# A lightweight convolution and a gated feed-forward: the first 1024 tokens convolved with channels as output partitions

## The chip, the cores and the metric

The kernel runs on one core of one Trainium2 chip. The metric is the device time of one execution in microseconds (us); the lower the better. Engines are named as in the profile: PE (TensorE matmuls), PEld (its weight loads), DVE (VectorE), ACT (ScalarE), POOL (GpSimd) and SP (SyncE, which here only issues DMAs).

## The reference

The input `x` has 8 batches of 4096 tokens with 192 channels. Each of 8 heads owns 24 channels and has 7 taps, made by a softmax. Every token becomes the weighted sum of itself and its six predecessors; then all 32768 tokens go through a gated feed-forward.

```python
w = weight - np.max(weight, axis=-1, keepdims=True)      # weight: (8, 7)
w = np.exp(w)
w = w / (np.sum(w, axis=-1, keepdims=True) + 1e-09)
x_pad = np.concatenate([np.zeros((B, 6, D)), x], axis=1)  # x: (8, 4096, 192)
idx = np.arange(S)[:, None] + np.arange(7)[None, :]
x_unf = x_pad[:, idx, :].reshape(B, S, 7, 8, 24)
y = np.einsum('hk,bskhg->bshg', w, x_unf).reshape(B * S, D)
gate = np.maximum(y @ w_gate, 0.0)                        # (192, 1536)
val = y @ w_val                                           # (192, 1536)
return (gate * val @ w_out).astype(np.float32)            # (1536, 192)
```

## The kernel before

The four pairs of batches (bp and bp + 4) go one after the other; in each pair the two batches are the two streams `st`, whose data lie on the lower and the upper 64 partitions. The unit of the feed-forward is a window of 512 tokens of both streams; a pair of batches has eight windows.

The convolution is a matmul with a band matrix: 118 tokens (112 and the 6 before them) in, 112 out, one 118 x 112 band for each head. The bands of heads 0 to 3 and 4 to 7 are two tiles, built at the start from the softmax (L163 to L201): DVE makes `prod` and `blk`, and ten small copies by DVE and ACT (L199, L201) put `blk` along the diagonals. Blocks of 112 tokens form groups: the first group of a batch has five, the others four. `load_x` (L88) brings one group of both streams into a tile `x_h` with GpSimd DMAs that turn fp32 into fp16; `xpool` has four such tiles, so a load waits for the convolution four groups earlier. The first tokens of a batch have no predecessors: a memset on DVE (L97) clears the rows ahead of them.

There are two forms of the convolution. `conv` (L255) has the band as the stationary operand: 8 matmuls (L266), one a head, whose output has tokens as partitions. ACT (three copies) and DVE (two) move it to a tile `y` (L279), and SP transposes each block by DMA (L298) into `xc`, which has channels as partitions, as the feed-forward needs it. `conv_first` (L215) serves only the first group of the program. It has `x_h` as the stationary operand in pieces of at most 32 channels, so that its output has channels as partitions at once: 120 matmuls (L238) into two PSUM tiles, then three copies to `xc` (L248 on ACT, L249 on DVE, L250 on ACT), and no transpose.

`gate_val` (L303) takes a window through 12 steps f of 128 hidden units each: 6 matmuls with Wg, 6 with Wv (L314), ReLU on ACT (L324), product on DVE (L325). `project` (L328) is 48 matmuls with Wo (L332), a copy by ACT (L340) and a store by SP (L342), for one stream of one window. PSUM holds four tiles of two banks each (`ps`), taken in turn by all of these.

The order is written out by hand. Windows go in twos: both `gate_val`, then the four `project`, and a `conv` after each `project` as long as a later window needs it, with a load of x behind it. In the first window two `conv` calls stand ahead of steps f = 4 and f = 8:

```python
            if bp == 0 and w == 0 and f in (4, 8):
                conv(0, f // 4)
```

The weights are needed on both halves of the partitions. A DMA brings them to the lower half in four slices of 384 hidden units (`load_w`, L141), a copy doubles them into the upper half (`both_halves`, L148): slice 0 on DVE, slices 1 to 3 on POOL. All these DMAs, all loads of x and the load of Wo (L364) are issued by POOL, in the order of the program, with its copies among them:

```python
    load_w(0)
    load_w(1)
    xts[1] = load_x(0, 1)
    load_w(2)
    xts[2] = load_x(0, 2)
    load_w(3)
    for s in range(1, NPART):
        both_halves(nc.gpsimd, s)
```

At the very start, while nothing is loaded yet, PE runs 24 matmuls on zeros (L77).

Of the kernel before, what the change touches and what calls it, by code (L numbers as in the profile page):

```python
# [8 lines left out]
FP = mybir.dt.float32  # L9
F16 = mybir.dt.float16  # L10
# [5 lines left out]
def kernel(  # L16
# [12 lines left out]
    nc = tc.nc  # L29

    B, S, D = x.shape
    H, KW = weight.shape
    G = D // H
    DFF = moe_w_gate.shape[1]
    PAD = KW - 1
    NB = B // 2
    NCH = D // 64
    NBLK = D // 32
    NFF = DFF // 128
    WIN = 512  # L40
    NWIN = S // WIN
    SUB = 112
    NSUB = (S + SUB - 1) // SUB
    GSUB = 5
    SUBS = [list(range(GSUB))] + [list(range(j, j + 4)) for j in range(GSUB, NSUB, 4)]
    NGRP = len(SUBS)

    ctx.enter_context(tc.manual_schedule())
    const = ctx.enter_context(tc.tile_pool(name="const", bufs=1))
    xpool = ctx.enter_context(tc.tile_pool(name="xpool", bufs=4))  # L50
    ypool = ctx.enter_context(tc.tile_pool(name="ypool", bufs=3))
    xcpool = ctx.enter_context(tc.tile_pool(name="xcpool", bufs=2))
# [2 lines left out]
    opool = ctx.enter_context(tc.tile_pool(name="opool", bufs=3))  # L55
    psum = ctx.enter_context(tc.tile_pool(name="psum", bufs=4, space=bass.MemoryType.PSUM))


    HH = H // 2
    wr = const.tile([128, HH, KW], FP)  # L60
    for half, eng in ((0, nc.sync), (1, nc.scalar)):
        eng.dma_start(
            out=wr[64 * half : 64 * half + 64],
            in_=bass.AP(
                tensor=weight.tensor,
                offset=weight.offset + half * HH * KW,
                ap=[[0, 64], [KW, HH], [1, KW]],
            ),
# [4 lines left out]
    zeros = const.tile([128, 512], F16)  # L73
    nc.vector.memset(zeros[:], 0.0)  # L74
    ps = psum.tile([128, 2, 512], FP, name="ps")
    for n in range(24):
        nc.tensor.matmul(  # L77
            out=ps[:, n % 2, :], lhsT=zeros[:, 0:128], rhs=zeros[:], start=True, stop=True
        )
# [2 lines left out]
    for half in range(2):  # L82
        nc.vector.memset(bands[half][:], 0.0)  # L83


    TOK = [min(SUB * j, S - SUB) for j in range(NSUB)]

    def load_x(bp, g):  # L88


        subs = SUBS[g]
        xt = xpool.tile([128, GSUB, 2, D], F16, name="x_h")
        for st in range(2):
            b = bp + NB * st
            jj = 0
            if g == 0:
                nc.vector.memset(xt[0:32, 0, st, :], 0.0)  # L97
                nc.gpsimd.dma_start(out=xt[PAD:128, 0, st, :], in_=x[b, 0 : 128 - PAD, :])  # L98
                jj = 1
            last = subs[-1] == NSUB - 1  # L100
            n_full = len(subs) - jj - int(last)
            lo = TOK[subs[jj]] - PAD
            src = bass.AP(
                tensor=x.tensor,
                offset=x.offset + (b * S + lo) * D,
                ap=[[D, 128], [SUB * D, n_full], [1, D]],
            )
            nc.gpsimd.dma_start(out=xt[:, jj : jj + n_full, st, :], in_=src)  # L108
            if last:
                nc.gpsimd.dma_start(  # L110
                    out=xt[0 : SUB + PAD, len(subs) - 1, st, :], in_=x[b, S - SUB - PAD : S, :]
                )
        return xt, subs

    xts = {}
    xts[0] = load_x(0, 0)


    eye = const.tile([128, 32 + KW], FP)
    for half in range(2):  # L120
        nc.gpsimd.affine_select(  # L121
            out=eye[64 * half : 64 * half + 64],
            in_=ones[64 * half : 64 * half + 64],
# [9 lines left out]
    Wg = const.tile([128, NCH, DFF], F16)  # L133
    Wv = const.tile([128, NCH, DFF], F16)
    Wo = const.tile([128, NFF, D], F16)
    NPART = 4
    FS = DFF // NPART

    def load_w(s):
        for src, dst in ((moe_w_gate, Wg), (moe_w_val, Wv)):  # L140
            nc.gpsimd.dma_start(  # L141
                out=dst[0:64, :, FS * s : FS * (s + 1)],
                in_=src.rearrange("(c p) f -> p c f", p=64)[:, :, FS * s : FS * (s + 1)],
            )

    def both_halves(eng, s):
        for dst in (Wg, Wv):
            eng.tensor_copy(  # L148
                out=dst[64:128, :, FS * s : FS * (s + 1)], in_=dst[0:64, :, FS * s : FS * (s + 1)]
            )  # L150

    load_w(0)
    load_w(1)
    xts[1] = load_x(0, 1)
    load_w(2)
    xts[2] = load_x(0, 2)
    load_w(3)
    for s in range(1, NPART):
        both_halves(nc.gpsimd, s)


    mx = const.tile([128, HH, 1], FP)
# [20 lines left out]
        out=prod[:],  # L183
# [9 lines left out]
    for half in range(2):  # L193
        for n, (r0, b0, b1, s0) in enumerate(places):
            ncol = min(32, SUB - s0)
            src = blk[64 * half + b0 : 64 * half + b1, :, 0:ncol, 0]
            dst = bands[half][r0 : r0 + b1 - b0, :, s0 : s0 + ncol]
            if n % 2 == half:
                nc.vector.tensor_copy(out=dst, in_=src)  # L199
            else:  # L200
                nc.scalar.copy(out=dst, in_=src)  # L201

    def band(h):
        return bands[h // HH][0 : SUB + PAD, h % HH, :]

    both_halves(nc.vector, 0)

    xc = {}

# [2 lines left out]
    PLACE = {0: (0, 0, 0), 1: (0, 0, 1), 3: (0, 1, 0), 4: (0, 1, 1)}  # L212
    PLACE |= {6: (1, 0, 0), 7: (1, 0, 1), 2: (1, 1, 0), 5: (1, 1, 1)}

    def conv_first():  # L215


        xt, subs = xts.pop(0)
        xc[0] = xcpool.tile([128, NCH, S], F16, name="xc")
        n = 4  # L220
        rows = SUB + PAD
        pa = psum.tile([128, 2, 512], FP, name="ps")
        pb = psum.tile([128, 2, 512], FP, name="ps")
        places = [(pa, 0), (pa, 1), (pb, 0)]
        for c in range(NCH):
            for jj in range(GSUB):
                if jj < n:
                    ps, bank, col = *places[c], SUB * jj
                else:
                    ps, bank, col = pb, 1, SUB * c  # L230
                for second in range(2):
                    for st in range(2):
                        for k2 in range(2):
                            k = 2 * c + k2
                            h0, h1 = 32 * k // G, (32 * k + 31) // G
                            h, m = (h0, G * h1 - 32 * k) if second else (h1, 32)
                            p0 = 64 * st + 32 * k2
                            nc.tensor.matmul(  # L238
                                out=ps[p0 : p0 + m, bank, col : col + SUB],
                                lhsT=xt[0:rows, jj, st, 32 * k : 32 * k + m],  # L240
                                rhs=band(h),
                                start=True,
                                stop=True,
                                tile_position=(0, p0),
                                skip_group_check=True,
                            )
            if c == 1:
                nc.scalar.copy(out=xc[0][:, 0:2, 0 : n * SUB], in_=pa[:, :, 0 : n * SUB])  # L248
        nc.vector.tensor_copy(out=xc[0][:, 2, 0 : n * SUB], in_=pb[:, 0, 0 : n * SUB])  # L249
        nc.scalar.copy(  # L250
            out=xc[0][:, :, n * SUB : GSUB * SUB],
            in_=pb[:, 1, 0 : NCH * SUB].rearrange("p (c t) -> p c t", c=NCH),
        )

    def conv(bp, g):  # L255


        xt, subs = xts.pop(NGRP * bp + g)
        if g == 0:
            xc[bp] = xcpool.tile([128, NCH, S], F16, name="xc")  # L260
        n = len(subs)
        rows = SUB + PAD
        W = 2 * n * G
        pair = [psum.tile([128, 2, 512], FP, name="ps") for _ in range(2)]
# [29 lines left out]
        move(nc.scalar.copy, 1, 0, 0, 0, 2, 16, G, G)  # L294
        move(nc.vector.tensor_copy, 1, 1, 0, 8, 0, 48, 2 * 128 - 48, 16)
        move(nc.vector.tensor_copy, 1, 1, 16, -16, 1, 0, 56, 8)
        for jj, j in enumerate(subs):
            nc.sync.dma_start_transpose(  # L298
                out=xc[bp][:, :, TOK[j] : TOK[j] + SUB],
                in_=y[0:SUB, jj].rearrange("p c s r -> p (c s r)"),  # L300
            )

    def gate_val(bp, w):  # L303
        h = hpool.tile([128, NFF, 2, WIN], F16, name="hT")
        xcb = xc[bp]
        for f in range(NFF):
            if bp == 0 and w == 0 and f in (4, 8):
                conv(0, f // 4)
            pss = []
            for W in (Wg, Wv):  # L310
                ps = psum.tile([128, 2, 512], FP, name="ps")
# [33 lines left out]
        )  # L345


    groups = [(bp, g) for bp in range(NB) for g in range(NGRP)]
    need = []
    for bp in range(NB):  # L350
        for w in range(NWIN):
            sub = (WIN * (w + 1) - 1) // SUB
            need.append(NGRP * bp + next(g for g in range(NGRP) if sub in SUBS[g]))
    wins = [(bp, w) for bp in range(NB) for w in range(NWIN)]
    loaded = 3
    conv_first()
    done = 3
    for i in range(0, len(wins), 2):
        last = need[min(i + 4, len(wins) - 1)]
        while loaded <= min(last, done + 3):  # L360
            xts[loaded] = load_x(*groups[loaded])
            loaded += 1
        if i == 0:
            nc.gpsimd.dma_start(out=Wo[:], in_=moe_w_out.rearrange("(c p) d -> p c d", p=128))  # L364
        pair = [(*wins[i + j], gate_val(*wins[i + j])) for j in range(2)]
        for bp, w, h in pair:
            for st in range(2):
                project(bp, w, h, st)
                if done <= last and done < loaded:
                    conv(*groups[done])  # L370
                    done += 1
                    if loaded <= last:
                        xts[loaded] = load_x(*groups[loaded])
                        loaded += 1


# [28 lines left out]
```

## Time and profile before

| | |
|---|---|
| median of 3 runs | 805.76 us (805.64 to 806.78) |
| the profiled execution: time, span | 806.04 us, 804.1 us |
| mean granted TensorE clock | 0.994 |
| PE busy | 791.8 us (98%), 8104 matmuls |
| DVE busy, ACT busy, POOL busy | 498.7 us (62%), 487.7 us (61%), 76.1 us (9%) |
| L314 matmuls (gate and val) | 4608 |
| L332 matmuls (projection) | 3072 |
| L266 matmuls (`conv`) | 280 |
| L238 matmuls (`conv_first`) | 120 |

All times within the profile are microseconds from the span's start. Matmuls overlap in the array, so the duration of one is longer than the distance to the next; distances are read from the starts. The granted clock is a share of full speed. The time of an execution is somewhat longer than its span, which goes from the first to the last instruction. The span of a DMA issue on POOL is the time in which the engine writes its descriptors; the transfer itself ends later ("landing").

### The profile page before, as it was taken

What the parts mean: (1) busy time and instruction counts of PE and PEld (TensorE: products, weight loads), DVE (VectorE), ACT (ScalarE), POOL (GpSimd) and SP (SyncE); (2) the same over time, 40 slices, a digit from 0 to 9 for tenths busy, and PEclk for the clock granted to TensorE, in tenths of its full rate; (3) what the DMA queues carried; (4) which work ended last, traced back from release to release, by engine and by line L of the source; (5) the groups of instructions that cost most, each with busy time, mean ns of one, the idle gap of its engine ahead of it and who ended that gap; (6) DMA issues with size and microseconds to landing.
All of it is one profiled execution on the core that took longest, in us unless ns stands there. A gap on an engine that the chain in (4) does not pass through costs nothing.

```text
span 804.1 us, 18844 instructions
## 1 busy us (share of the span) xinstructions
PE 791.8 (98%) x8104; PEld 523.6 (65%) x8104; DVE 498.7 (62%) x482; ACT 487.7 (61%) x562; POOL 76.1 (9%) x109
## 2 busy tenths in 40 slices
PE   8799999999999999999999999999999999999997
PEld 3367494765947658485674947658485584856647
DVE  5663928659195682937749295591946839386490
ACT  3565737567475664747657375574747657375571
POOL 8401020000201002010010100201010010000000
PEclk9999999999999999999999999999999999999999
DMA  9909036160913209252090511908156070210202
GB/s 124 140 11 161 5 80 99 33 128 1 139 53 54 81 1 124 56 73 86 20 170 2 90 45 30 150 2 114 45 59 133 2 133 1 66 49 23 75 1 79
DMA packets 129170, 54.97 MB, mean 68 GB/s; under 512 B 94784, under 2 KB 129088, under 8 KB 129088
## 3 DMA queue, kind: packets, MB, share of 16 engines
q1 hardware_dynamic: 86496, 37.50, 20.2%
q0 software_dynamic: 42512, 16.28, 19.3%
q8 instruction: 63, 1.03, 0.5%
q14 instruction: 19, 0.16, 0.1%
q10 hardware_dynamic: 80, 0.01, 0.0%
HBM read 32.55 MB, written 25.17 MB: 72 GB/s over the span
## 4 chain that ended last, share of the span: by engine, by line
PE 97%; DMA 2%; POOL 0%; DVE 0%; ACT 0%; issue 0%; POOLq 0%; ACTq 0%
PE ps L314 62%; PE ps L332 32%; PE ps L266 3%; DMA xc<-y 1%; DMA Wv<-in_moe_w_val_dram 1%; POOL x_h L108 0%; POOL x_h L98 0%; ACT out_s L340 0%; DVE xc L249 0%; POOL Wg L141 0%; DVE Wv L148 0%; DVE band L83 0%; POOL eye L121 0%; ACT xc L250 0%; DVE zeros L74 0%
## 5 line engine op out<-in xcount | busy, mean ns | idle before, releaser
L325 DVE TENSOR_TENSOR hT<-gr,ps 128x1024 f16<-128x1024 f16 x384 | 468.9, 1221 | 142.0 <-ACT gr L324 107.1
L324 ACT ACTIVATE gr<-ps 128x1024 f16<-128x1024 f32 x384 | 392.8, 1023 | 108.2 <-PE ps L314 108.2
L314 PE MATMUL ps<-xc,Wg 64*128 64x512 f16 x2304 | 313.9, 378 | 6.3 <-DMA xc<-y 4.2
L314 PE MATMUL ps<-xc,Wv 64*128 64x512 f16 x2304 | 313.3, 378 | 0.0
L332 PE MATMUL ps<-Wo,hT 128*128 128x192 f16 x3072 | 261.7, 246 | 0.0
L332 PEld LDWEIGHTS <-hT 128*128 128x128 f16 x3072 | 253.2, 98 | 6.8 <-issue 6.8
L314 PEld LDWEIGHTS <-Wv 64*128 64x128 f16 x2304 | 130.7, 94 | 119.8 <-issue 2.4
L314 PEld LDWEIGHTS <-Wg 64*128 64x128 f16 x2304 | 112.0, 94 | 141.7 <-issue 8.3
L340 ACT COPY out_s<-ps 128x768 f32<-128x768 f32 x64 | 51.1, 798 | 195.5 <-PE ps L332 184.6
L279 DVE CAST y<-ps 112x256 f16<-112x256 f32 (+1 forms) x70 | 22.1, 357 | 139.0 <-ACT y L279 138.8
L108 POOL DMA_DIRECT2D x_h<-in_x_dram x72 | 54.1, 762 | 412.9 <-PE ps L266 373.2
L279 ACT CAST y<-ps 112x384 f16<-112x384 f32 (+1 forms) x105 | 44.2, 500 | 0.2
L266 PE MATMUL ps<-x_h,band 118*112 118x192 f16 (+1 forms) x280 | 29.7, 248 | 0.0
L266 PEld LDWEIGHTS <-band 118*112 118x112 f16 x280 | 25.2, 130 | 1.0 <-issue 0.8
L98 POOL DMA_DIRECT2D x_h<-in_x_dram x8 | 4.5, 556 | 155.9 <-issue 154.3
L77 PE MATMUL ps<-zeros 128*128 128x512 f16 x24 | 7.9, 503 | 1.3 <-DVE zeros L74 1.3
L77 PEld LDWEIGHTS <-zeros 128*128 128x128 f16 x24 | 2.8, 122 | 5.8 <-issue 3.4
L110 POOL DMA_DIRECT2D x_h<-in_x_dram x8 | 4.6, 572 | 0.0
L148 POOL COPY Wg<-Wg 64x1152 f16<-64x1152 f16 x3 | 3.4, 1141 | 1.7 <-DMA Wg<-in_moe_w_gate_dram 1.7
L148 POOL COPY Wv<-Wv 64x1152 f16<-64x1152 f16 x3 | 3.4, 1141 | 0.0
L201 ACT COPY band<-blk 64x128 f16<-64x128 f16 (+2 forms) x5 | 1.4, 284 | 3.3 <-DVE blk L190 3.2
L141 POOL DMA_DIRECT2D Wg<-in_moe_w_gate_dram x4 | 2.6, 640 | 0.0
(29 smaller groups left out, 18.6 us busy)
## 6 DMA issues: line engine op xcount, KB each, us to landing
out_dram<-out_s SPq DMA_DIRECT2D x64, 384.0 KB, 3.0
x_h<-in_x_dram POOLq DMA_DIRECT2D x64, 192.0 KB, 5.7
xc<-y SPq DMA_TRANSPOSE x143, 3.8
x_h<-in_x_dram POOLq DMA_DIRECT2D x8, 144.0 KB, 4.6
Wg<-in_moe_w_gate_dram POOLq DMA_DIRECT2D x4, 144.0 KB, 6.2
Wv<-in_moe_w_val_dram POOLq DMA_DIRECT2D x4, 144.0 KB, 6.3
Wo<-in_moe_w_out_dram POOLq DMA_DIRECT2D x1, 576.0 KB, 13.3
x_h<-in_x_dram POOLq DMA_DIRECT2D x8, 45.8 KB, 3.9
```

Source lines behind the costliest of these rows:

```text
L77: nc.tensor.matmul(out=ps[:, n % 2, :], lhsT=zeros[:, 0:128], rhs=zeros[:], start=True, stop=True)
L98: nc.gpsimd.dma_start(out=xt[PAD:128, 0, st, :], in_=x[b, 0 : 128 - PAD, :])
L108: nc.gpsimd.dma_start(out=xt[:, jj : jj + n_full, st, :], in_=src)
L110: nc.gpsimd.dma_start(out=xt[0 : SUB + PAD, len(subs) - 1, st, :], in_=x[b, S - SUB - PAD : S, :])
L148: eng.tensor_copy(out=dst[64:128, :, FS * s : FS * (s + 1)], in_=dst[0:64, :, FS * s : FS * (s + 1)])
L266: nc.tensor.matmul(out=pair[t][0:SUB, bank, W * slot : W * (slot + 1)], lhsT=band(h), rhs=xt[0:rows, 0:n, :, G * h : G * (h + 1)], start=True,
L279: copy(out=bass.AP(tensor=dst.tensor, offset=dst.offset + 128 * c + r0, ap=[dst.ap[0], [step_out, 2], [NCH * 128, n], [64, 2], [1, width]] ...
L314: nc.tensor.matmul(out=ps[:, st, :], lhsT=W[64 * st : 64 * st + 64, c, 128 * f : 128 * (f + 1)], rhs=xcb[64 * st : 64 * st + 64, c, WIN * ...
L324: nc.scalar.activation(out=gr[:], in_=pss[0][:], func=ACTF.Relu)
L325: nc.vector.tensor_tensor(out=h[:, f], in0=gr[:], in1=pss[1][:], op=ALU.mult)
L332: nc.tensor.matmul(out=ps[:, q // 2, D * (q % 2) : D * (q % 2) + D], lhsT=h[:, f, st, 128 * q : 128 * (q + 1)], rhs=Wo[:, f, :], start=(f ...
L340: nc.scalar.copy(out=os_[:], in_=ps[:, :, 0 : 2 * D])
```

## The change

- The first two windows (1024 tokens) of the first pair of batches become two groups of five blocks, at tokens 0 and 512; the fifth block of each gives only 64 tokens. Both go through `conv_dense`, which is `conv_first` with three PSUM tiles, one for each piece of 64 channels, each copied to `xc` as soon as its 40 matmuls are issued (ACT, DVE, ACT). From token 1024 on groups of four follow as before.
- `conv_dense(1)` stands ahead of f = 8 of the first window, where `conv` was called; the call ahead of f = 4 is gone. `conv(2)` comes after the first two `gate_val`.
- The weights come in five slices of 128, 256, 384, 384 and 384 hidden units. Slices 0 and 1 are doubled by DVE, within `conv_dense(0)`: slice 0 ahead of its copies, slice 1 behind them. Slices 2 to 4 are doubled by POOL, and the issues of slice 4 and of later x stand between these copies.
- The load of the first group is issued ahead of everything else, with the large DMAs ahead of the small ones, and one memset in place of two.
- 18 matmuls on zeros at the start in place of 24, and three more between `conv_dense(0)` and the first window.
- Of the ten copies for the bands DVE takes pieces 0, 2, 4 of both halves and ACT pieces 1 and 3; before, the second half was the other way round.
- The loop at the end loads x as far ahead as before, through a helper `ahead()`.

```diff
-    SUBS = [list(range(GSUB))] + [list(range(j, j + 4)) for j in range(GSUB, NSUB, 4)]
+    GROUPS = []
+    for bp in range(NB):
+        if bp == 0:
+            for w in range(2):
+                GROUPS.append((bp, [WIN * w + SUB * j for j in range(GSUB)]))
+        at = GROUPS[-1][1][0] + WIN if bp == 0 else 0
+        starts = [min(t, S - SUB) for t in range(at, S, SUB)]
+        head = len(starts) % 4 or 4
+        cuts = [0] + list(range(head if head != 1 else GSUB, len(starts) + 1, 4))
+        GROUPS += [(bp, starts[i:j]) for i, j in zip(cuts, cuts[1:])]
...
+    xts = {}
+    xts[0] = load_x(0)
...
-    for n in range(24):
+    for n in range(18):
         nc.tensor.matmul(
             out=ps[:, n % 2, :], lhsT=zeros[:, 0:128], rhs=zeros[:], start=True, stop=True
         )
...
-    xts = {}
-    xts[0] = load_x(0, 0)
...
-    NPART = 4
-    FS = DFF // NPART
+    CUTS = [0, 128, 384, 768, 1152, DFF]
...
-    load_w(0)
-    load_w(1)
-    xts[1] = load_x(0, 1)
-    load_w(2)
-    xts[2] = load_x(0, 2)
-    load_w(3)
-    for s in range(1, NPART):
-        both_halves(nc.gpsimd, s)
+    def pool_halves(s):
+        both_halves(nc.gpsimd.tensor_copy, s, Wg)
+        both_halves(nc.gpsimd.tensor_copy, s, Wv)
+
+    for s in range(4):
+        load_w(s)
+    xts[1] = load_x(1)
+    pool_halves(2)
+    load_w(4)
+    pool_halves(3)
+    xts[2] = load_x(2)
+    pool_halves(4)
...
-            if n % 2 == half:
+            if n % 2 == 0:
                 nc.vector.tensor_copy(out=dst, in_=src)
             else:
                 nc.scalar.copy(out=dst, in_=src)
...
-    both_halves(nc.vector, 0)
...
+        if g == 0:
+            both_halves(nc.vector.tensor_copy, 0, Wg)
+            both_halves(nc.vector.tensor_copy, 0, Wv)
         for c in range(NCH):
+            ps = psum.tile([128, 2, 512], FP, name="ps")
             for jj in range(GSUB):
...
-                                out=ps[p0 : p0 + m, bank, col : col + SUB],
+                                out=ps[p0 : p0 + m, 0, col : col + n],
                                 lhsT=xt[0:rows, jj, st, 32 * k : 32 * k + m],
-                                rhs=band(h),
+                                rhs=band(h)[:, 0:n],
...
+            copy = nc.vector.tensor_copy if c == 1 else nc.scalar.copy
+            copy(out=xc[0][:, c, t0 : t0 + WIN], in_=ps[:, 0, :])
         if g == 0:
+            both_halves(nc.vector.tensor_copy, 1, Wg)
+            both_halves(nc.vector.tensor_copy, 1, Wv)
...
-            if bp == 0 and w == 0 and f in (4, 8):
-                conv(0, f // 4)
+            if bp == 0 and w == 0 and f == 8:
+                conv_dense(1)
...
-    conv_first()
-    done = 3
+    conv_dense(0)
+    ps = psum.tile([128, 2, 512], FP, name="ps")
+    for n in range(3):
+        nc.tensor.matmul(
+            out=ps[:, n % 2, :], lhsT=zeros[:, 0:128], rhs=zeros[:], start=True, stop=True
+        )
+    done = 2
...
         pair = [(*wins[i + j], gate_val(*wins[i + j])) for j in range(2)]
+        if i == 0:
+            conv(done)
+            done += 1
```

## The prediction

> **What bounds the kernel now.** I read the page first, for the engine that sets the time, and the chain that ended last.
>
> ```profile
> PE 791.8 (98%) x8104; PEld 523.6 (65%) x8104; DVE 498.7 (62%) x482; ACT 487.7 (61%) x562; POOL 76.1 (9%) x109
> PE 97%; DMA 2%; POOL 0%; DVE 0%; ACT 0%; issue 0%; POOLq 0%; ACTq 0%
> ```
>
> TensorE (PE) is the path for 97% of the span: only fewer or faster matmuls, or fewer holes between them, can pay. The waits of PE come next; columns are total, times, longest, in us.
>
> ```profile
> PE ps L314 <- DMA xc<-y: 4.2, 1, 4.2
> PE ps L314 <- ACT xc L250: 2.1, 1, 2.1
> PE ps L77 <- DVE zeros L74: 1.3, 1, 1.3
> ```
>
> Three holes, all early; asked from 100 to 800 us the same view is empty. The rest of the program is a solid row of matmuls that the change hardly touches. Where the holes lie, and what led to them, the chain in order of time shows (start, length, what):
>
> ```profile
> 6.07 5.22 DMA Wv<-in_moe_w_val_dram
> ...
> 11.31 0.55 DVE Wv L148
> ...
> 11.89 0.64 DVE xc L249
> ...
> 12.55 0.45 ACT xc L250
> ...
> 13.04 7.04 PE ps L314 x48
> 20.09 0.92 PE ps L266 x8
> ...
> 29.41 7.12 DMA xc<-y
> ...
> 36.67 17.42 PE ps L314 x144
> 54.09 4.07 PE ps L332 x48
> ```
>
> Hole one: the first window (512 tokens) starts at 13.04 because the weight slice Wv lands at 11.29, VectorE (DVE) copies it, and only then evicts part of `xc`. Hole two: the second window starts at 36.67 because its `xc` comes by DMA transpose. Last I asked for short stretches (us, PE busy, PEld, DVE, ACT, POOL, granted clock, DMA share, GB/s):
>
> ```profile
> 12.00:14.00 2.00, 0.96 (x6) 0.47 (x7) 0.52 (x1) 0.44 (x1) 1.86 (x4) 0.81 1.47 176
> 14.00:16.00 2.00, 2.00 (x12) 0.90 (x10) 0.25 (x1) 1.02 (x1) 1.93 (x2) 0.50 1.39 197
> 16.00:18.00 2.00, 2.00 (x20) 0.91 (x17) 1.03 (x2) 1.02 (x1) 1.41 (x2) 0.84 1.53 193
> ...
> 38.00:40.00 2.00, 2.00 (x12) 0.83 (x10) 0.89 (x1) 0.78 (x1) 0.00 (x0) 0.50 1.48 181
> ```
>
> After each hole the granted clock is 0.50 for a while: a hole costs more than its length. One feed-forward step f (12 matmuls of 512 columns) takes 1.30 us at full clock: f4 to f7 start at 20.93, 22.24, 23.54, 24.83. After hole one, f0 and f1 take 13.04 to 17.32, 4.28 us for 2.60; after hole two 36.67 to 40.94, 4.27 for 2.60. So each hole adds 1.68 of half clock.
>
> **The change, part by part.** The sum goes against the profiled execution: span 804.1, time 806.04, so 1.94 lies around the span; the median of the three runs, 805.76, is 0.28 below it.
>
> *Start of the first dense convolution.* The 24 zero matmuls run from 1.31 to 9.16 and PE takes the convolution at 9.09, so today they hold it. In the timeline the first 12 go at 0.427 apart, the last 11 at 0.205 (2.26 for 11). Eighteen are 12 x 0.427 + 6 x 0.21 = 6.4, ending at about 7.9 (`load_x`'s memset now precedes theirs on DVE: +0.2). Then the band binds. Its copies start at 7.73; the new assignment gives DVE pieces 0, 2, 4 of the lower half first (0.28 + 0.19 + 0.17), ACT 1 and 3 (2 x 0.30): lower band complete at about 8.4. The first 40 matmuls need only that half; the upper one is complete at about 9.0, when the next 40 ask. The tokens are in time: POOL's first DMA waited until 2.13 for a memset in the same tile; the large loads now come first and touch other columns of it. If they start at about 0.9, four issues (0.79, 0.79, 0.55, 0.55) and the two eye selects (0.54) end at 4.2, not 5.4; were they to wait for the memset, 0.4 of that is lost. Convolution: 8.45.
>
> *Its end.* 120 matmuls took 1.82 (L238, 9.09 to 10.91), so 10.25. Each of the three PSUM tiles is evicted as soon as it is full: ACT took 0.91 for 896 columns and 0.44 for 336, so 0.59 for 512; DVE 0.62 for 448, so 0.70. Tiles fill at 9.05, 9.65, 10.25; evictions end at about 9.7, 10.4, 10.9, if DVE is free at 9.7. Ahead of its eviction stand the copies of slice 0 (128 of 384 columns: a third of 0.55, 0.2 each). Wv0 is issued at 4.8 instead of 6.07; with the old landing of 5.2 it is there at 10.0 and the DVE eviction ends at 11.0; as it is a third of the bytes I take 9. The three added zero matmuls (0.64) fill PE until 10.9. The first window therefore starts at 10.9, and at full clock, as no stretch of a microsecond is empty before it: gain 2.14 + 1.68.
>
> *Slices 1 to 4 within the window.* Step f runs at 10.9 + 1.3f. POOL issues at 0.63 each: slice 1 until 6.7, 2 until 8.0, 3 until 9.2, x of group 1 until 10.8. Slice 1 (f1, f2) at the longest old landing for early slices, 6.3, is there at 12.4; two DVE copies of 0.4, one done before; f1 wants Wv at 12.85: even. Slice 2 (f3 to f5, wanted 14.8 and 15.45): landing between 4.7 (12.1) and 7.5 (14.9), two POOL copies of 1.14: ready 14.3 or 17.1 at the ends. I take about 13.5, because fewer bytes precede it (the old slice 1, also second in the queue, was awaited by nobody), and keep 1.6 for the range. Everything behind these copies on POOL waits with them: slice 4's issues (until 14.8), slice 3's copies (17.1; f6 at 18.7), x of group 2 (18.6), slice 4's copies (20.9; f9 at 24.4), three groups of x (4.5 us), and Wo at 25.6. Wo landed 13.3 after its issue: 38.9; the first projection asks at about 44.9.
>
> *The convolutions in the windows.* Removed: two `conv` calls in window 0, 0.92 each. Added: `conv_dense(1)` at f8, 1.82 (its evictions, 0.59 x 2 on ACT and 0.70 on DVE, lie beside the matmuls; PSUM tiles come back before f8 needs them), and `conv(2)` after the pair, 0.80 (between 0.66 and 0.92 in the chain). Net -0.78. All later calls stay 33 in number, as do their places.
>
> *Hole two goes.* Window 1 reads PSUM evictions of f8, four steps earlier: gain 4.17 + 1.67. What is late next? Transposes for window 2: `conv(3)` still stands behind the first projection, but SP now issues `conv(2)`'s four (5.1 us) ahead: its own begin at about 52.5 and the one that window 2 needs lands 4.2 to 5.9 later, by 58.5; window 2 starts at 62.7. Covered.
>
> Sum: 2.14 + 1.68 + 4.17 + 1.67 - 0.78 = 8.9. Span 795.2, time 797.1 against this profile, 796.9 against the median. Adding up by position instead (10.9 + 24 x 1.30 + 1.82 + 0.80 = 44.7, where 54.09 stands now) gives 9.4; the difference is the seams between steps, and I take the smaller.
>
> The Trainium skill has two rules that speak against it. *TensorE: Matmul & The Clock Gate* (Part 1) says that the clock is released and gated by free-running windows of about 3.4 us, and gated after an idle one. Here 2.14 us of wait sufficed for 0.50, so the row is stricter than the rule; by the rule a start with fewer zeros could miss a window, and the sum would be 8.9 - 1.7 = 7.2, by the rows it is 8.9. *DMA: Bandwidth & Descriptors* (Specifications) asks for 512 B for line rate, while slice 0 writes rows of 128 fp16, 256 B. If the rule doubled the time of so small a slice (an estimate from that page), it would still be there before the added zeros end, and the sum would stay 8.9; no row of before has such rows.
>
> **The rivals.**
>
> *A transfer is late in window 0 or the start is cold* (17%). Slice 2 late by 1.6, or x of group 1, which f8 wants at 21.3: issued by 10.8, at the longest x landing of 13.7 it comes at 23.7 to 24.5, a hole of 3.2 and 1.7 of half clock. For: the DMA engines are at 1.4 to 1.5 of 2 in those rows. Against: that landing stood behind Wo and transposes. A cold start costs 1.7. Gain 4 to 7.2: 798.6 to 802.
>
> *The second dense group saves nothing* (2%): if `xc` is ordered as a whole, f8 and window 1 could still wait for other writers of it. Hole two and its clock stay: gain 3.0, 802.8; with hole one kept too, within 0.2% of 805.76. Against: today f4 to f11 of window 0 run while transposes write other columns of `xc`.
>
> *POOL's queue* (3%, slower). Slice 4's DMAs now stand behind copies that wait for slice 2, its copies behind x loads. One late landing shifts all. Slice 4 is ready at 20.9, wanted at 24.4; every us beyond costs one, plus 1.7 of clock. Break-even at 24.4 + 8.9 - 1.7 = 31.6; slower by 0.2% from 33.2: a shift of 12.3, so 811 at a shift of 16. For: 13.7 has been seen once. Against: POOL waited 1.7 for weights in all, and the longest weight landing is 7.5.
>
> *Better than forecast* (3%): the seams (0.5), shorter dense calls (the fifth block has 64 columns, 0.15 each), a start at 10.6: down to 795.
>
> **How the numbers follow.** The forecast with its own spread of 1.5 has 75%: 795.4 to 798.4. The range 795.0 to 800.2 adds half of the late-transfer case. About 0.2%, 1.6 us, is what a measurement of this kernel can tell from no change. Faster by more: 0.75 + 0.17 + 0.03 = 0.95; within: 0.02, the second rival with both holes kept; slower: 0.03.
>
> **What would show it.** PE's waits without `xc<-y`; granted clock 1.00 from 10 to 20 us; L314 from about 10.9; projections from about 45; solid PE after. Wrong: a wait of PE on Wg, Wv, x or Wo, a stretch of 0.50 after 10 us, or a later pair longer than now.

## The result and the profile after

The changed kernel takes 796.58 us (median of 4 runs, 796.44 to 797.48) beside 805.70 for the kernel before (median of 4, 804.0 to 806.78): a ratio of 0.9891, 95% interval 0.9872 to 0.9910. The forecast was 796.9 in a range of 795.0 to 800.2. Its profiled execution has a span of 794.7, 9.4 less than the 804.1 before.

The page's lines on the busy time of each engine, and on the chain by engine:

```profile
PE 788.0 (99%) x8213; PEld 523.2 (66%) x8213; DVE 499.4 (63%) x480; ACT 487.9 (61%) x560; POOL 77.4 (10%) x111
PE 98%; DVE 0%; DMA 0%; ACT 0%; issue 0%; DVEq 0%; ACTq 0%
```

PE was busy for 791.8 of 804.1, now for 788.0 of 794.7: the idle part fell from 12.3 to 6.7 and the busy part by 3.8, although there are more matmuls. Some matmuls had run slower before. The waits of PE (total, times, longest):

```profile
PE ps L118 <- DVE zeros L115: 1.5, 1, 1.5
PE ps L247 <- DVE band L210: 0.5, 1, 0.5
```

Both holes are gone; what is left is the first memset and a half microsecond for the band. The chain in order of time (start, length, what), and the short stretches whose column before the last two is the granted clock:

```profile
8.47 1.61 PE ps L247 x109
10.08 0.76 PE ps L364 x3
10.84 10.47 PE ps L322 x96
...
23.04 20.88 PE ps L322 x192
43.93 0.91 PE ps L274 x8
44.84 3.96 PE ps L340 x48
```

```profile
12.00:14.00 2.00, 2.00 (x22) 0.91 (x18) 1.23 (x2) 1.68 (x2) 2.00 (x3) 1.00 1.25 151
14.00:16.00 2.00, 2.00 (x22) 0.99 (x21) 1.93 (x2) 1.50 (x2) 2.00 (x4) 1.00 1.54 189
...
38.00:40.00 2.00, 2.00 (x22) 1.07 (x20) 1.93 (x2) 1.59 (x2) 0.00 (x0) 1.00 0.00 0
```

From 8.47 on PE waits for nothing, and the clock is 1.00 where it was 0.50. The first projection starts at 44.84 instead of 54.09: 9.25 of the 9.4 lie ahead of it. What follows is as long as before (750.0 and 749.9).

### The profile page after: what moved, and what is told of

It reads as the page before. It is cut to its first block, busy times and chain, and to the rows that moved or that the text cites. A ratio compares the mean times of both kernels' runs of the same rounds, so it can differ in the third digit from the quotient of the medians.

```text
span 794.7 us, 19044 instructions
## 1 busy us (share of the span) xinstructions
PE 788.0 (99%) x8213; PEld 523.2 (66%) x8213; DVE 499.4 (63%) x480; ACT 487.9 (61%) x560; POOL 77.4 (10%) x111
## 3 DMA queue, kind: packets, MB, share of 16 engines
q1 hardware_dynamic: 85024, 37.15, 20.9%
## 4 chain that ended last, share of the span: by engine, by line
PE 98%; DVE 0%; DMA 0%; ACT 0%; issue 0%; DVEq 0%; ACTq 0%
PE ps L322 63%; PE ps L340 32%; PE ps L274 3%; PE ps L247 0%; DMA wr<-in_weight_dram 0%; DVE prod L193 0%; DVE blk L201 0%; ACT out_s L348 0%; PE ps L364 0%; DVE band L210 0%; ACT we L179 0%; DVE we L176 0%; DVE we L184 0%; DVE mx L174 0%; DVE sm L181 0%
## 5 line engine op out<-in xcount | busy, mean ns | idle before, releaser
L332 ACT ACTIVATE gr<-ps 128x1024 f16<-128x1024 f32 x384 | 393.3, 1024 | 100.5 <-PE ps L322 100.5
L247 PEld LDWEIGHTS <-x_h 118*32 118x32 f16 (+3 forms) x240 | 3.0, 93 | 1.5 <-issue 1.5
L247 PE MATMUL ps<-band,x_h 118*32 118x112 f16 (+7 forms) x240 | 3.4, 209 | 0.5 <-DVE band L210 0.5
```

Of the source, the lines that this page charges most:

```text
L247: nc.tensor.matmul(out=ps[p0 : p0 + m, 0, col : col + n], lhsT=xt[0:rows, jj, st, 32 * k : 32 * k + m], rhs=band(h)[:, 0:n], start=True, s ...
L332: nc.scalar.activation(out=gr[:], in_=pss[0][:], func=ACTF.Relu)
```

## The experiments

Each run is compared with runs of the kernel before on the same chip; in the three comparisons below that kernel had medians of 804.87 (23 runs), 804.74 (7) and 805.0 (6).

### The second dense group alone

```diff
 # the changed kernel, with the start of the kernel before
-    for n in range(18):
+    for n in range(24):
-    CUTS = [0, 128, 384, 768, 1152, DFF]
+    CUTS = [0, 384, 768, 1152, DFF]
...
+                if c == 1:
+                    nc.scalar.copy(out=xc[0][:, 0:2, 0:WIN], in_=pa[:])
+                if c == 2:
+                    nc.vector.tensor_copy(out=xc[0][:, 2, 0:WIN], in_=pb[:, 0, :])
```

> Only the second dense group: the start (24 zero matmuls, four weight slices, order of loads and of POOL's copies, band pieces, two PSUM tiles for the first group) is as before; the first group gives 512 tokens instead of 560. My sum: hole two and its half clock go (4.17 + 1.67), a dense call of 1.82 and conv(2) of 0.80 replace two calls of 0.92: gain 5.1, and up to 0.4 more because the third copy of the first group is gone; 800.2 to 800.9, PE waits only once, near 12 to 13. Rival 'the start is what counts': less than 2 us of gain.

Measured 797.53 (797.18 to 798.03), ratio 0.991 (0.9888 to 0.9932): 7.3 less than before, 2 more than I expected. Waits of PE:

```profile
PE ps L329 <- DVE xc L264: 0.8, 1, 0.8
PE ps L329 <- ACT xc L262: 0.7, 1, 0.7
```

Hole one has split: four matmuls on channels 0 to 127 run between two waits, and the others of the first window begin at 12.54. In this profile the granted clock stays 1.00 through it, so the 1.68 of half clock that my sum had left behind hole one is missing. The old start, measured here without its half clock, is only 0.95 slower than the new one (797.53 and 796.58).

### The start alone

```diff
-            for w in range(2):
+            for w in range(1):
                 GROUPS.append((bp, [WIN * w + SUB * j for j in range(GSUB)]))
...
-            if bp == 0 and w == 0 and f == 8:
-                conv_dense(1)
+            if bp == 0 and w == 0 and f in (4, 8):
+                conv(f // 4)
```

> Only the start of the change: window 1 again comes by conv and DMA transposes ahead of f4 and f8; all else as in the changed kernel. My sum: first window at 10.8 at full clock, gain 2.2 + 1.68 = 3.9, hole two stays with 4.2 and its half clock: 801.8. With the second window's share of 5.1 the two parts then add up to the whole, 9.1. Rival 'parts are not additive': an earlier first window meets the DMAs of the weights, the hole grows by what was won, and the gain is under 2.

Measured 803.54 (801.41 to 804.51), ratio 0.9976 (0.9959 to 0.9992): a gain of 1.3. That is the rival's number and not my 3.9, but it is not the rival's mechanism: the first window started at 10.84, as expected, and the hole did not grow. Its waits, then the stretches behind hole two:

```profile
PE ps L322 <- DMA xc<-y: 4.0, 1, 4.0
...
PE ps L274 <- DMA x_h<-in_x_dram: 0.3, 1, 0.3
```

```profile
32.00:34.00 2.00, 1.13 (x6) 0.51 (x8) 0.00 (x0) 0.00 (x0) 0.00 (x0) 0.50 1.42 178
34.00:36.00 2.00, 2.00 (x12) 0.88 (x10) 0.27 (x1) 1.02 (x1) 0.00 (x0) 0.50 1.45 179
36.00:38.00 2.00, 2.00 (x14) 0.76 (x10) 0.95 (x1) 1.02 (x1) 0.00 (x0) 0.50 1.60 190
```

The clock is 0.50 from within the hole until about 38; steps f0 and f1 take from 32.87 to 37.95, 5.08 for 2.60. Half clock cost 2.5 here, not 1.67. Less 0.8 for that, and less the 1.68 behind hole one, which two further profiles of the kernel before (below) do not show, my 3.9 comes to 1.4; this account rests on one profile. The gains of the two parts, 7.3 and 1.3, add up to 8.6 beside 8.3 for the whole (804.87 to 796.58).

### The holes filled, the waits kept

```diff
 # the kernel before
     conv_first()
+    fill(9)
     done = 3
...
+        if bp == 0 and w == 1:
+            fill(18)
         for f in range(NFF):
```

`fill` runs that many matmuls on zeros into a PSUM tile of its own.

> The kernel before with 9 zero matmuls in hole one (9 x 0.21 = 1.9 of 2.14) and 18 in hole two (3.8 of 4.17): the waits stay, only the idle time of PE is filled. If the half clock after a hole is the price of an idle PE, the granted clock stays at 1.00 and the time falls by the two terms of 1.68 and 1.67 to 802.4. If it comes from the waits' cause (DMA, evictions) and not from idleness, the time stays at 805.7.

Measured 802.29 (12 runs, 801.74 to 802.83), ratio 0.9969 (0.9956 to 0.9981). The stretch that holds the end of the filling:

```profile
32.00:34.00 2.00, 2.00 (x11) 0.94 (x10) 0.44 (x1) 0.00 (x0) 0.00 (x0) 1.00 1.45 181
34.00:36.00 2.00, 2.00 (x18) 0.75 (x18) 0.00 (x0) 0.45 (x1) 0.00 (x0) 1.00 1.45 179
```

Useless work makes the kernel 2.6 faster, and its 12 times spread by 1.1 where the 23 of the kernel before spread by 6.5 (801.96 to 808.46). The time met my first reading, and the DMAs and evictions are still there: the half clock is the price of an idle PE. From the median of 804.87, though, both terms would have made 3.4, not 2.6. The next two profiles give a reason.

### The kernel before, two more profiles

No edit.

> The kernel before, unaltered, once more with a profile, since its single times went from 801.96 to 808.46 while the changed kernel's stay within 1.1. If the length of the half clock after the holes is what varies, the holes stay at about 2.1 and 4.2 and the start of the first projection moves with the time, by 0 to 3.4 a hole: 802.0 with none, 805.4 with two of 1.7. If the holes themselves vary, the waits of PE move and the clock rows do not.

> As the run before it, a third profile of the kernel before: the same two readings, with the sum of waits and half clock accounting for the difference between the two times within 0.3.

They took 805.35 and 803.21. Waits of PE in the one, then in the other:

```profile
PE ps L314 <- DMA xc<-y: 5.1, 1, 5.1
PE ps L314 <- ACT xc L250: 2.6, 1, 2.6
```

```profile
PE ps L314 <- DMA xc<-y: 3.3, 1, 3.3
PE ps L314 <- ACT xc L250: 1.8, 1, 1.8
```

The stretches of the first behind hole one and behind hole two (the column before the last two is the granted clock):

```profile
14.00:16.00 2.00, 2.00 (x22) 1.03 (x18) 1.08 (x1) 1.73 (x2) 1.93 (x2) 1.00 1.41 193
...
36.00:38.00 2.00, 2.00 (x12) 0.94 (x10) 0.00 (x0) 0.76 (x1) 0.00 (x0) 0.50 1.42 177
```

Both readings hold in part. The holes vary: the second by 1.8, and the first window starts at 13.01 and 12.63; these two differences, 2.2, account for the 2.1 between the times. The sum of the waits does not: the first wait is 0.8 longer in the one profile, but half of that lies ahead, where its dense group ended 0.4 earlier. And the clock varies: neither profile shows 0.50 behind hole one (four steps in 5.36), both do behind hole two (f0 and f1 in 4.27 and 4.28). So in three profiles of this kernel half clock followed hole one once and hole two three times, and hole two was 3.3, 4.2 and 5.1 long. What made 808.46 was not profiled.

### The number of zero matmuls

```diff
-    for n in range(18):
+    for n in range(8):      # the other run: 24
```

> The changed kernel with 8 zero matmuls at the start instead of 18: they end at 4.9, and PE idles until the band at 8.5. If the clock needs recent activity, the first dense group (1.6 longer) and f0, f1 (up to 2.6 longer) run at half clock: 798.2 to 800.5. If 18 were more than it needs: 796.6.

> The changed kernel with the 24 zero matmuls of before: they end at 9.1 to 9.3, the first dense group starts 0.6 to 0.8 later than 8.5, and all behind it: 797.2 to 797.4. If the clock is released earlier and they end before 8.6: 796.6.

With 8: 799.29 (798.31 to 799.58), as in the first case. Its timeline (start, length):

```profile
9.10 2.75 PE L247 MATMUL ps<-band,x_h 118*32 118x112 f16 x120 [4.00 <-DVE band L210]
11.78 1.46 PE L364 MATMUL ps<-zeros 128*128 128x512 f16 x3
```

The dense group takes 2.75 instead of 1.61, three zeros 1.46 instead of 0.82; f0 and f1 are nearly at full pace. The first projection starts 2.5 later than in the second profile of the changed kernel (47.42 and 44.93): these two pieces make 1.8 of it, and a band that came 0.56 later, for a reason given below, most of the rest. Yet the row of granted clocks says 1.00 here: in these profiles it does not show the slow pace in which an execution begins. That pace is read from the distances of the matmuls.

With 24: 796.96 (796.52, 796.85, 797.07 and 797.53), beside 796.54 for the changed kernel in another comparison. The four reach from the second of my readings to a little above the first. The profiled one is the fastest: there the clock was released early and all 24 ended by 8.3, ahead of the band, as in the second reading. Whether the zeros held the slower ones was not profiled.

### Without the three added zeros, and channels first

```diff
-    for n in range(3):
-        nc.tensor.matmul(
-            out=ps[:, n % 2, :], lhsT=zeros[:, 0:128], rhs=zeros[:], start=True, stop=True
-        )
```

> The changed kernel without the three zero matmuls after the first dense group. Theory 1: they only occupy PE until the last eviction (10.73); without them the first matmuls on channels 0 to 127 run ahead of it and the first window ends 0.3 to 0.5 earlier at full clock: 796.1 to 796.3 where the changed kernel has 796.6. Theory 2: they keep the clock; without them the granted clock falls to 0.5 for a window of some 3.4 us after 10 and the time is 798.3.

> The changed kernel without the three added zero matmuls, and step f0 of the first window taking channels 0 to 127 of gate and val first, channels 128 to 191 of both last. If the last eviction (about 10.75) bounds the first window, PE has 8 matmuls to do ahead of it: f0 ends at 11.5 instead of 12.07, 796.0. If PE or the weights bound it, no gain: 796.6.

> The changed kernel unaltered, beside the next three on the same chip: 796.6, first window at 10.8 if the DMA of the softmax weights lands as before (the softmax starts at 3.85); at 11.4 and 0.6 longer if it lands as late as in the run without added zeros (4.46).

796.64 without them (796.26 to 796.77), 796.63 with the channels reordered too (796.35 to 797.29), 796.54 for the changed kernel, unaltered (796.47 to 796.54). Theory 2 is out: the clock stays 1.00. Counted from the first dense matmul to the first projection it is 35.93 without them (9.10 to 45.03) and 36.39 with them (8.54 to 44.93), a gain within the 0.3 to 0.5 of theory 1. But in both kernels without them the softmax starts at 4.46 instead of 3.94, because its weights land later, and this takes the gain back. With the channels reordered f0 ended only 0.13 earlier (12.13 and 12.26), and PE then waited twice 0.2 for DVE's products. Neither version beat the changed kernel.

### Four weight slices

```diff
-    CUTS = [0, 128, 384, 768, 1152, DFF]
+    CUTS = [0, 384, 768, 1152, DFF]
...
-    pool_halves(2)
-    load_w(4)
-    pool_halves(3)
+    pool_halves(1)
+    load_w(3)
+    pool_halves(2)
```

> The changed kernel with four slices of 384 hidden units, slice 0 doubled by DVE ahead of the evictions, slices 1 to 3 by POOL. My step: Wv0 lands 5 us after its issue at 5.2, at 10.2; two copies of 0.55; DVE's eviction ends near 11.5 instead of 10.4, the first window starts 0.7 to 1.0 later: 797.3 to 797.6. Rival 'small slices cost as much as they bring': 796.6.

Measured 797.89, but from 796.62 to 800.69 (ratio 0.9915, 0.9883 to 0.9948): the median is near my step, but two of the four runs took 796.62, the rival's time, so they do not settle it. The profiled run (799.15) shows a cost I had not reckoned with. DVE, then POOL:

```profile
10.36 1.43 DVE L157 COPY Wg<-Wg 64x1152 f16<-64x1152 f16 x1
11.72 1.29 DVE L157 COPY Wv<-Wv 64x1152 f16<-64x1152 f16 x1
13.04 0.69 DVE L257 CAST xc<-ps 128x512 f16<-128x512 f32 x1
```

```profile
10.24 1.14 POOL L157 COPY Wg<-Wg 64x1152 f16<-64x1152 f16 x1
11.33 1.27 POOL L157 COPY Wv<-Wv 64x1152 f16<-64x1152 f16 x1
```

The two DVE copies, 0.55 each before, took 1.43 and 1.29 while POOL copied, and the eviction behind them ended at 13.7. Each ended 0.41 after the POOL copy beside it (11.79 after 11.38, 13.01 after 12.60), as if it had stood still until then. In the changed kernel slice 0's copies are done by 9.46, ahead of POOL's first at 11.35. Two other things made this execution slow: DVE's copies for the bands began 0.9 later (8.64 and 7.72) and took 0.5 longer (1.69 and 1.22).

### The first load as before

```diff
-    xts = {}
-    xts[0] = load_x(0)
...
     for half in range(2):
         nc.vector.memset(bands[half][:], 0.0)
+    xts = {}
+    xts[0] = load_x(0)
```

and in `load_x` the small DMA of each stream ahead of its large one.

> The changed kernel with the first load of x placed and ordered as before (after the memsets, small DMAs first). Two runs with that order had PE wait for x until 8.99 and 9.33; the first dense group then starts 0.5 to 0.9 later than 8.47, and the weights are issued 0.9 later: 797.2 to 797.6. If the tokens had slack, as I reckoned in the prediction, only the weights count: 796.6 to 796.8.

Measured 797.05 (796.85 to 798.09), 0.5 above the changed kernel. Waits of PE:

```profile
PE ps L245 <- ACT band L210: 0.7, 1, 0.7
PE ps L245 <- DMA x_h<-in_x_dram: 0.3, 1, 0.3
```

The median lies between my two readings, and the waits decide for the first: the tokens do bind in the old order, until 9.08, and the first window starts at 11.20 instead of 10.86, less than I had expected. The new order of the band copies and the third PSUM tile were not taken out singly.

## Why the prediction was right, and where it was not

**The sum.** Against the profiled execution each term came out:

| step | predicted | measured | from |
|---|---|---|---|
| dense group starts | 8.45 | 8.47 | chain |
| evictions end | 9.7, 10.4, 10.9 | 9.75, 10.38, 10.73 | timeline |
| first window starts | 10.9 | 10.84 | chain |
| half clock, both holes | 1.68 + 1.67 gone | clock 1.00 | stretches |
| hole two | 4.17 gone | no such wait | waits |
| second dense group, `conv(2)` | 1.82, 0.80 | 1.74, 0.91 | chain |
| slices 2, 3, 4 ready | 13.5, 17.1, 20.9 | 13.58, 17.04, 20.75 | timeline |
| Wo issued | 25.6 | 25.07 | timeline |
| first projection | 44.9 | 44.84 | chain |

The terms of my sum give 2.20 + 1.68 + 4.17 + 1.67 - 0.81 = 8.9; the chain moved by 9.25. The rest is the seams that I had set aside: four steps between two `conv` calls took 5.29, four of the sixteen after the change 5.22. Adding up by position, 9.4, was closer.

**POOL's queue and Wo.** The slower rival needed a shift of 12.3 on POOL; there was none, and PE waited neither for slice 2 nor for the tokens of group 1. The profile gives Wo a landing of 9.6 after its issue, so at 34.7, ten ahead of its use, where I had reckoned 38.9. That no transposes ran in that stretch fits; no run tests it.

**The small slices.** The first load began at 1.31 and not at 0.9, so slice 0 was issued at 4.56 and 5.21. It landed 3.0 and 2.6 later, at about 7.6 and 7.8, where I had taken 9, and was copied at 8.98 and 9.19, as soon as DVE was free. The Trainium skill asks for 512 B for line rate (*DMA: Bandwidth & Descriptors*, Specifications). What the 256 B rows cost cannot be told here, as nothing waited for them. My estimate by that page was also wrong in itself: the 4.2 that the sum gave slice 0 (4.8 to 9), doubled, ends at 13.2, behind the added zeros and not ahead of them. And rows below 512 B are nothing new: x is written in rows of 192 fp16, 384 B, and of the 129170 packets of the kernel before the profile counts 94784 under 512 B.

**A reason that was wrong.** "Today they hold it", said of the zero matmuls, is true of two of three profiles of the kernel before: in one more they ran until 9.21 and the dense group began at 9.14. In the other all 24 ended by 8.6 and the dense group began at 8.53. With the holes filled it began early, at 8.38, and then waited for x until 9.33. Fewer zeros therefore help in an execution where the clock is released late. Where it is released early the earlier load of x can help instead, as that wait shows. My step gave all of it to the zeros. The 8.45 itself came out because the band set it, as the prediction had said.

**A term that is a draw.** I took 1.68 of half clock for each hole as fixed. It followed hole one in one profile of three, and its size behind hole two was 1.67, 1.67, 1.68 before, but 2.5 with the start alone. The 4.17 of hole two is one draw from 3.3 to 5.1. Against the typical execution of the kernel before (804.87 in the largest set) the gain is 8.3, not 9.1, and the shares differ: the second dense group brings 7.3 and the new start on top of it 0.95, where my sum had 5.1 and 3.8. Which waits would go was right: the lists of waits after the change, and with each part alone, show it. That 8.9 came so close to the measured 9.1 is partly luck: the sum went against a profiled execution that had paid for both half clocks.

**The load order has a price.** In all six profiles with the old order of the first load the softmax starts between 3.78 and 3.85. With x issued first it starts between 3.85 and 3.94 in four, and between 4.46 and 4.63 in the other four; the band and all behind it follow. The prediction did not ask whom the earlier transfers would meet. That the DMAs of x delay the small one of the softmax weights fits, but whether it goes by program or by draw stays open.

**The clock rule.** The Trainium skill (*TensorE: Matmul & The Clock Gate*, Part 1) has free-running windows of about 3.4 us, gated after an idle one. The draw behind hole one, and the 8 zeros (3.4 us of matmuls) that left the pace at half, can be read by such windows, though no run shows where they lie. That waits of 2.1 and 3.3, shorter than a window, were followed by 0.50 goes against the rule: here less than a whole idle window sufficed.

## What to carry to other kernels

A hole in a matmul stream costs its length and then, not in every execution, some microseconds of half clock; look at the clock behind each hole, and profile more than once before giving a share to it. Adding up by position along the chain caught the seams that a sum of differences missed. An engine that copies ahead of an eviction delays it by whatever slows the copy, its neighbour's copies included.

## What the runs showed of the hardware

- A DVE copy of 64 x 1152 fp16 from SBUF to SBUF took 0.55 to 0.75 with no POOL copy beside it and 1.29 to 1.43 beside one of the same size; POOL's took 1.14 to 1.27. One of 64 x 768 took 0.40 to 0.53 without and, with 8 zeros, 1.35 beside a POOL copy.
- 120 matmuls, 96 of 112 columns and 24 of 64, into 32-column pieces of the array took 1.61, 13 ns apart, though most are recorded as lasting some 213 ns.
- The granted clock reads 1.00 at the start of an execution while matmuls of 512 columns are 0.43 apart, against 0.21 later.
- Filling two holes with matmuls on zeros took 2.6 off the median and cut the spread of the times from 6.5 (23 runs) to 1.1 (12 runs).
